# A spectral filter, a GELU block and a layer norm on one core: six filter loads instead of three ahead of the first DMA transpose, fewer throwaway matmuls, and the bias column behind the first tile's copy

## Chip, core and metric

The kernel runs on one core of a Trainium2 chip. The metric is the device time of one execution in microseconds (us). A profiled execution has a span, from its first to its last instruction, and a time of its own that is somewhat longer.

The engines are named as in the profile: PE (TensorE, matrix products, with its weight loads PEld), DVE (VectorE), ACT (ScalarE), POOL (GpSimd) and SP (SyncE, which here only issues DMAs). SBUF is the on-chip memory, PSUM the eight banks into which PE writes.

## The reference

```python
x = A_x                                  # 1 x 2048 x 640, bf16
xn = _layernorm(x, axis=-1)
return x + _A_ref(xn, A_w_r, A_w_i) + _B_ref(xn, B_w1, B_b1, B_w2, B_b2)

def _A_ref(x, w_r, w_i):                 # filter in the frequency domain
    X = jnp.fft.rfft2(x.astype(jnp.float32), axes=(-2, -1))
    X = X * (w_r + 1j * w_i)             # weights 2048 x 321
    return jnp.fft.irfft2(X, s=(S, D), axes=(-2, -1)).astype(jnp.bfloat16)

def _B_ref(x, w1, b1, w2, b2):           # 640 -> 1536 -> 640
    h = jnp.einsum("bsd,df->bsf", x, w1) + b1
    h = _gelu(h)
    return jnp.einsum("bsf,fd->bsd", h, w2) + b2
```

Both branches read the same normalized `xn`, and their sum is added to `x`.

## The kernel before

The 2048 rows are 16 tiles (c = 0 to 15) of 128 rows. Each tile is loaded (`load_x`), its mean and variance are taken on DVE (L584, L588), and the normalized tile is made on DVE (L617, into a buffer that the profile calls Z or T). Two users follow.

*The dense branch.* `xn` is needed with rows and columns exchanged (`xnT`). Tiles 0 to 3 and 5 to 7 are transposed on PE (L635) and copied out of PSUM by ACT or DVE (L496, L497). Tile 4 and tiles 8 to 15 (`BYDMA`) are transposed by a DMA that SP issues (L624). Then come the products with w1, in blocks of tiles (0), (1), (2, 3), (4 to 7), (8 to 11), (12 to 15) and 12 column groups each (`hps` in the code, L483 `ps<-xnT,W` in the profile); w1 comes in three loads (`W1P`: groups 0 to 2, 3 to 6 and 7 to 11). ACT adds the bias column `b1col` and takes the gelu (L688). The products with w2 (`ps<-W,gT`) come late in the kernel; w2 comes in four loads.

*The spectral branch* is a Fourier transform written as matrix products with tables (G, E, M, N, GE, H). The first stage uses `gtab`, the second (`bps`) `etab`, the third (`cps`) the matrix M on 32x32 tiles (`ps<-Xb,mtab`). Its results Y are copied out of PSUM by ACT and DVE, two copies each for each half, and are multiplied on DVE with the filter weights in `Wf` (four products T on L756, four sums Z on L760 for a pair of row groups). The first inverse stage (`dps`, `ps<-Z,ntab`) takes the Z; its results U are transposed by DMA (L781) into `XV`, from where the last stages run. `cps`, `dps` and the last stage's `eps` use PSUM banks 0 to 3, four at a time.

*The filter weights* come in 34 loads on SP, 17 of w_r first and then 17 of w_i. Most have 80.2 KB; the second and the third of each half have 10.0 and 70.2 KB, since one row stands alone. Every filter product on DVE waits for all 34.

*Order.* The program writes no order by hand. Each step is an operation with the engines that may do it, a price in us, a priority, what it reads and writes, and sometimes a gate (not before that step has started) or a due time `late` (not before that moment on the planner's clock). `Sched.schedule` runs through this as a list scheduler: at each point the engine that can start earliest takes, among what it can start within 0.03, the step of the highest priority. The prices and due times set the order of each engine's queue, the engine of a step that two may do, and its PSUM bank; they are not waited for on the chip. There every engine runs its queue in that order and waits for semaphores only. DMA transposes have priority 500 and more or less by a table (`DELTA`), loads on SP 400.

`load` (L478) gives the prices of DMA issues: 0.6 for a filter load, 1.0 on POOL, 0.45 for all others. The due time of the k-th filter load is

```python
late=WLATE[0] + WLATE[1] * len(B_w.writers)      # WLATE = (14.6, 0.72)
```

On SP this makes the order: loads of x, b1, w1 and G; three filter loads; the transpose of tile 4; thirteen filter loads; transposes 8 and 9; two filter loads; transposes 10 to 13; one w2 load; one filter load; transposes 14 and 15; one w2 load; the last fifteen filter loads; two w2 loads; H; then the transposes of U and the stores.

*The front.* While the first tile comes in, PE runs `WARM[0]` = 46 matmuls on zeros whose result nobody reads (`idle`, `ps<-warm`). After the five transposes of tile 0 it runs one small matmul that turns b1 into a column (`b1ps`), which ACT copies into `b1col` (L640), and `WARM[1]` = 6 more throwaway matmuls. ACT and DVE copy tile 0's transposed columns out of PSUM (`EVAC`: three fifths ACT, two fifths DVE), and block 0 of the dense branch starts.

Of the kernel before, what the change touches and what calls it, by code (L numbers as in the profile page):

```python
# [9 lines left out]
ACT = mybir.ActivationFunctionType  # L10
# [3 lines left out]
D = 640  # L14
# [4 lines left out]
NFC = 12  # L19
# [80 lines left out]
def act_us(n, ptr=0):  # L100
    return 0.055 + n / 1200.0 + 0.09 * ptr
# [277 lines left out]
W1P = ((0, 3), (3, 7), (7, 12))  # L379
GROUPS = ((0, 2), (2, 3), (5, 3), (8, 3), (11, 3), (14, 2))  # L380
BYDMA = (4, 8, 9, 10, 11, 12, 13, 14, 15)
WLATE = (14.6, 0.72)
ANY = [(0, 8)]
ZONE = {'hps': [(4, 8)], 'bps': [(0, 4), (4, 8)], 'cps': [(0, 4)], 'dps': [(0, 4)], 'eps': [(0, 4)], 'fin': [(0, 8)], 'fps': [(4, 8)], 'tps': [(0, 8)], 'aps': [(0, 8)]}
PRIO = {'hps': -118.5, 'gelu': -251.6, 'pb': 89.9, 'pc': 206.3, 'filt': 461.0, 'ipc': 165.5, 'eps': 24.1, 'fin': -47.0}
# [5 lines left out]
RES = 261.9  # L391
W2LATE = (31.0, 2.4)
HLATE = 59.8
WARM = (46, 6)
X2POS = 2
FLAG = 1.4
EVAC = {0: [((0, 3), "act"), ((3, 5), "dve")], 1: [((0, 3), "act"), ((3, 5), "dve")]}
# [2 lines left out]
def bass_parallel_sum__spectral_gfnet__dense_activation_gelu__prompt_kernel(  # L400
# [20 lines left out]
    K = Sched(nc, ["sp", "pe", "act", "dve", "pool"])  # L421
    with ExitStack() as es:
# [11 lines left out]
        ident = sb("ident", [128, 128])  # L434
# [7 lines left out]
        b1t = sb("b1t", [NFC, 128])  # L442
        b1col = sb("b1col", [128, NFC], F32)
# [11 lines left out]
        xnT = sb("xnT", [128, 5, S])  # L455
# [14 lines left out]
        def psb(slot, dims, off=0, p0=0, n=128):  # L470
            return bass.AP(tensor=PS, offset=p0 * 4096 + slot * 512 + off, ap=[[4096, n]] + dims)
# [3 lines left out]
        p_yo, p_y2, p_yf, p_os = Pool(2), Pool(1), Pool(2), Pool(4)  # L475

        def load(dst, src, buf, nbytes, after=(), reads=(), rate=395e3, q="sp", late=0.0):
            return K.op([(q, 0.6 if buf is B_w else 1.0 if q == "pool" else 0.45)], 20 if q == "pool" else 400, lambda e, _: e.dma_start(dst, src), reads=reads, writes=[buf], after=after, nbytes=nbytes, rate=rate, late=late)  # L478

        def mms(lst):  # L480
            def f(e, _):
# [5 lines left out]
        def pe(segs, prio, lst, **kw):  # L487

            o = K.op([("pe", sum(u for _, u in segs))], prio, mms(lst), alts=[segs], **kw)
            o.lst = lst  # L490
            return o
# [24 lines left out]
        B_id, B_b1, B_b2b = Buf("ident"), Buf("b1t"), Buf("b2")  # L516
# [3 lines left out]
        B_w2 = [Buf(f"w2_{j}") for j in range(4)]  # L520
        B_w = Buf("W")
# [50 lines left out]
        B_b1ps, B_b1c = Buf("b1ps", psum), Buf("b1col")  # L572
# [5 lines left out]
        for c0, n in [(0, 1), (1, 1)] + [(c, 2) for c in range(2, 16, 2)]:  # L578
            pr = 100 - c0 / 2
            B_mv, B_ve, B_r = Buf("mv"), Buf("ve"), Buf("r")  # L580
            for c in range(c0, c0 + n):
                B_st = Buf("st")
                for h in range(2):
                    st = K.op([("dve", 0.393)], pr, lambda e, _, c=c, h=h: e.bn_stats(stats[:, c, 6 * h:6 * h + 6], view(X, c * D + H2 * h, [[1, H2]])),  # L584
                         reads=[B_x[c]], writes=[B_st], gate=first_ve if c == 1 else [])
# [9 lines left out]
            else:  # L595
                K.op([("dve", 0.09)], pr, lambda e, _, a=a, b=b: e.tensor_scalar_add(ve[:, a:b], mv[:, a:b, 1], 1e-5), reads=[B_mv], writes=[B_ve])  # L596
                K.op([("pool", 0.65)], pr, lambda e, _, a=a, b=b: e.tensor_tensor(out=rstd[:, a:b], in0=ve[:, a:b], in1=mhalf[:, a:b], op=ALU.pow),  # L597
                     reads=[B_ve, B_mh], writes=[B_r])
# [3 lines left out]
        for pair in range(8):  # L602
            xn, x1, xf = Buf(f"xn{pair}", p_xn), Buf(f"xe{pair}", p_x1), Buf(f"xf{pair}", p_xf)

            def xnv(n, o, dims, xn=xn):
                return view((TT, Yb, Zb)[xn.slot // 2], xn.slot % 2 * 2 * D + n * D + o, dims)

            def x1v(o, dims, x1=x1):
                return view(TT, X1 + x1.slot * 2 * D + o, dims)

            def xfv(o, dims, xf=xf):
                return view(TT, XF + xf.slot * 2 * D + o, dims)
            for n in range(2):
                c = 2 * pair + n
                pr = 100 - c / 2
                B_xn = Buf(f"xn_{c}")
                o = K.op([("dve", 0.356)], pr, lambda e, _, c=c, n=n, xnv=xnv: e.tensor_scalar(  # L617
                    out=xnv(n, 0, [[1, D]]), in0=view(X, c * D, [[1, D]]), scalar1=mv[:, c, 0:1], scalar2=rstd[:, c:c + 1], op0=ALU.subtract, op1=ALU.mult),
                    reads=[B_x[c], B_rs[c]], writes=[xn, B_xn])
                norm_ops.append(o)  # L620
                if not c:
                    second_st.gate.append(o)
                if c in BYDMA:
                    K.op([("sp", 1.3)], 500, lambda e, _, c=c, n=n, xnv=xnv: e.dma_start_transpose(xnT[:, :, 128 * c:128 * c + 128], xnv(n, 0, [[1, D]])),  # L624
                         reads=[B_xn, xn], writes=[B_xnT[c]], nbytes=163840, rate=137e3)
                    continue
                tps = Buf(f"tps{c}", psum, 2 if c < 2 else 1, ZONE["tps"])

                def tpv(j0, j1, c=c, tps=tps):
                    over = c < 2 and j0 >= 3  # L630
                    return psb(tps.slot + over, [[1, 512]]).bitcast(BF)[:, 128 * (j0 - 3 * over):128 * (j1 - 3 * over)]

                def xt(e, _, n=n, xnv=xnv, tpv=tpv):
                    for j in range(5):
                        ins = e.transpose(tpv(j, j + 1), xnv(n, 128 * j, [[1, 128]]), ident[:])  # L635
                    return ins
                tp = K.op([("pe", 5 * mm_us(128))], pr, xt, reads=[B_xn, xn, B_id], writes=[tps], alts=[[("128", 5 * mm_us(128))]])
                if not c:
                    pe([("128", 0.1)], 200, lambda: [(psb(B_b1ps.slot, [[1, NFC]]), b1t[:], ident[0:NFC, 0:NFC], True, True)], reads=[B_b1, B_id], writes=[B_b1ps], gate=[tp])
                    K.op([("act", 0.2)], 200, lambda e, _: e.activation(b1col[:], psb(B_b1ps.slot, [[1, NFC]]), ACT.Copy), reads=[B_b1ps], writes=[B_b1c])  # L640
                    idle(WARM[1], WARM[1] * mm_us(128), gate=[tp])
                for k, (js, engs) in enumerate(EVAC[c] if c < 2 else [((0, 5), "both")]):
                    w = 128 * (js[1] - js[0])
                    K.op([x for x in (("dve", 0.066 + w / 1860.0), ("act", act_us(w))) if engs in ("both", x[0])], pr,
                         copy(lambda c=c, js=js: xnT[:, js[0]:js[1], 128 * c:128 * c + 128],
                              lambda tpv=tpv, js=js: tpv(*js).rearrange("p (j t) -> p j t", j=js[1] - js[0])),
                         reads=[tps], writes=[B_xnT[c]] + ([B_xnTp[c][k]] if c < 2 else []))
            pr = 100 - pair - FLAG
            for k, op in enumerate((ALU.add, ALU.subtract)):
                K.op([("dve", dve_us(640, 2))], pr, lambda e, _, k=k, op=op, xnv=xnv, x1v=x1v: e.tensor_tensor(  # L650
                    out=x1v(H2 * k, [[D, 2], [1, H2]]), in0=xnv(0, 0, [[D, 2], [1, H2]]), in1=xnv(0, D - 1, [[D, 2], [-1, H2]]), op=op), reads=[xn], writes=[x1])
            for k, op in enumerate((ALU.add, ALU.subtract)):
                for o_, o0, o1, w in ((128 * k, 0, H2 - 1, 128), (512 + 32 * k, 128, H2 - 129, 32)):
                    ring_ops.append(K.op([("dve", dve_us(4 * w, 2))], pr, lambda e, _, op=op, x1v=x1v, xfv=xfv, o_=o_, o0=o0, o1=o1, w=w: e.tensor_tensor(  # L654
                        out=xfv(o_, [[D, 2], [2 * w, 2], [1, w]]), in0=x1v(o0, [[D, 2], [H2, 2], [1, w]]), in1=x1v(o1, [[D, 2], [H2, 2], [-1, w]]), op=op),
                        reads=[x1], writes=[xf]))
            aps = Buf(f"aps{pair}", psum, 3, ZONE["aps"])
            for n in range(2):
                c = 2 * pair + n
                o = pe([("128", 5 * mm_us(128))], pr, lambda c=c, n=n, xfv=xfv, aps=aps: [  # L660
                    (psb(aps.slot, [[4, 64], [1, 2]], 256 * j + 2 * n), xfv(n * D + 128 * j, [[1, 128]]), gtab[:, 128 * c:128 * c + 128], True, True) for j in range(5)],
                    reads=[xf, B_g], writes=[aps])
                ring_ops.append(o)
                a_ops.append(o)
            for js in XASPLIT[pair]:
                K.op([("dve", dve_us(256 * len(js))), ("act", act_us(256 * len(js)))], pr,
                     copy(lambda pair=pair, js=js: view(XV, 2048 * js[0] + 4 * pair, [[2048, len(js)], [32, 64], [1, 4]]),
                          lambda aps=aps, js=js: psb(aps.slot, [[256, len(js)], [4, 64], [1, 4]], 256 * js[0])),
                     reads=[aps], writes=[B_xa[pair]])
# [3 lines left out]
        for bi, (c0, nt) in enumerate(BLOCKS):  # L673
            for fc in range(NFC):
# [4 lines left out]
                pr = PRIO["hps"] - bi - fc / 20  # L679
                w = [j for j, (a, b) in enumerate(W1P) if a <= fc < b][0]  # L680
                part_ = []
                for k, js in enumerate(((0, 1, 2), (3, 4))):
                    part_ = [pe([("128", len(js) * mm_us(128 * nt))], pr + 0.01 * len(part_), lambda c0=c0, nt=nt, fc=fc, hps=hps, js=js: [
                        (psb(hps.slot, [[1, 128 * nt]]), view(W1, F * j + 128 * fc, [[1, 128]]), xnT[:, j, 128 * c0:128 * (c0 + nt)], j == 0, j == 4) for j in js],
                        reads=[B_w1s[w]] + (B_xnTp[c0][:k + 1] if c0 < 2 else B_xnT[c0:c0 + nt]), writes=[hps], gate=part_)]
# [4 lines left out]
                    reads=[hps, B_b1c], writes=[bg])  # L690
# [18 lines left out]
        for gi, (c0, n) in enumerate(GROUPS):  # L709
# [4 lines left out]
                reads=B_xa + [B_e], writes=[bps, xb]))  # L714
# [9 lines left out]
        for P in range(4):  # L724
# [28 lines left out]
            for pair, Y, TB, Z in zip(two, Ys, TBs, Zs):  # L753
                pr = PRIO["filt"] - pair / 5
# [23 lines left out]
            for pair, U, B_u in zip(two, Us, B_us):  # L778
                for qq in range(2):
                    q = 2 * pair + qq  # L780
                    K.op([("sp", 1.3)], 500, lambda e, _, q=q, qq=qq, U=U, uv=uv: e.dma_start_transpose(  # L781
                        XV[:, :, 128 * q:128 * q + 128], uv(U, D * qq, [[1, D]])), reads=[U, B_u], writes=[B_v[q]], nbytes=163840, rate=137e3)

        for a, b in zip(CHAIN, CHAIN[1:]):
# [117 lines left out]
```

## Time and profile before

| | |
|---|---|
| median of 6 runs | 152.68 us (152.45 to 152.8) |
| profiled execution, its own time | 152.8 us |
| its span | 151.0 us |
| PE busy in the span | 144.5 us, 96% |
| DVE, ACT, POOL busy | 114.2, 80.9, 9.3 us |
| chain that ended last | PE 77%, DMA 8%, DVE 4%, SP queue 4%, ACT 3% |
| HBM read and written | 10.96 MB and 2.62 MB |

"Busy" of PE counts each matmul to a modelled end, and matmuls overlap, so 96% isn't a peak rate. The chain that ended last is followed back from the last instruction: at each step to what released it, or to the instruction before it on its engine; "issue" is time for which the profile shows no releaser. In a timeline a row is a run of equal instructions: start, length, engine, line, instruction, what it writes and reads, shape, how many, and in brackets the idle time before it and what ended that. SPq rows are DMA issues: their length is the time SP takes to issue, not the transfer; "us to landing" is from the issue to the completion.

### The profile page before, as it was taken

Reading aid. Unit: us, or ns where it says so; the run is one execution under the profiler, and the core shown is the slowest. Engines: PE = TensorE matmul, PEld = TensorE weight load, DVE = VectorE, ACT = ScalarE, POOL = GpSimd, SP = SyncE. Lnnn points to the kernel's source line nnn. Section 1 sums busy time; section 2 is a strip of 40 time slices with the busy share of each in tenths; the row PEclk is TensorE's granted clock in tenths of the full one; section 3 lists DMA queues with packets and bytes.
Section 4 is the critical chain, followed back from the end, with each engine's and each line's share of the span. In section 5 each row is a group of like instructions: output and inputs, shape, how many; then the busy total and the mean of one; then the engine's idle time right before and its main releaser. Section 6 shows DMA issues by size and latency. Waiting matters only on the chain.

```text
span 151.0 us, 4079 instructions
## 1 busy us (share of the span) xinstructions
PE 144.5 (96%) x1725; PEld 87.9 (58%) x1725; DVE 114.2 (76%) x244; ACT 80.9 (54%) x143; POOL 9.3 (6%) x22
## 2 busy tenths in 40 slices
PE   7989799999999997999999999999999999999993
PEld 7879697545556352355354455555667665655563
DVE  1999988999933569497999999942489998656433
ACT  3689979766886779678999471230124204100000
POOL 1120341124000000000000000000000000000000
PEclk9999999999999999999999999999999999999999
DMA  4999966658997575094006406205200232202022
GB/s 135 360 401 384 217 149 133 135 123 126 228 221 161 120 219 208 0 82 96 7 0 82 96 4 121 57 20 119 42 0 3 88 130 87 87 4 105 25 87 87
DMA packets 29610, 17.93 MB, mean 119 GB/s; under 512 B 18425, under 2 KB 28281, under 8 KB 29593
## 3 DMA queue, kind: packets, MB, share of 16 engines
q1 hardware_dynamic: 28552, 16.47, 43.7%
q0 software_dynamic: 240, 0.69, 1.7%
q10 hardware_dynamic: 800, 0.52, 1.2%
q8 instruction: 13, 0.21, 0.6%
q14 instruction: 5, 0.03, 0.1%
HBM read 10.96 MB, written 2.62 MB: 90 GB/s over the span
## 4 chain that ended last, share of the span: by engine, by line
PE 77%; DMA 8%; DVE 4%; SPq 4%; ACT 3%; issue 1%
PE ps L483 77%; DMA W<-in_B_w_dram 8%; SPq L478 4%; DVE T L756 2%; ACT gT L688 1%; DVE Z L760 1%; ACT T L496 1%; ACT U L496 1%; DVE Y L497 1%; DVE xnT L856 0%; ACT Y L496 0%; PE ps L635 0%; DVE W L865 0%
## 5 line engine op out<-in xcount | busy, mean ns | idle before, releaser
L483 PE MATMUL ps<-xnT,W 128*128 128x512 bf16 (+2 forms) x360 | 56.5, 308 | 1.4 <-DMA W<-in_B_w_dram 1.2
L483 PE MATMUL ps<-W,gT 128*128 128x512 bf16 (+3 forms) x396 | 56.0, 295 | 0.1
L483 PEld LDWEIGHTS ps<-W,gT 128*128 128x128 bf16 x396 | 30.1, 98 | 22.6 <-issue 1.2
L483 PEld LDWEIGHTS ps<-xnT,W 128*128 128x128 bf16 x360 | 28.8, 98 | 22.2 <-issue 2.1
L688 ACT ACTIVATE gT<-ps,b1col 128x512 bf16<-128x512 f32 (+2 forms) x72 | 36.3, 552 | 6.7 <-PE ps L483 6.2
L496 ACT ACTIVATE Wf<-ps 128x960 bf16<-128x960 f32 (+1 forms) x8 | 7.0, 902 | 23.7 <-PE ps L483 23.7
L584 DVE BATCH_NORM_STATS2 stats<-X 128x6 f32<-128x320 bf16 x32 | 14.1, 470 | 2.3 <-DMA X<-in_A_x_dram 2.3
L756 DVE TENSOR_TENSOR T<-Y,Wf 128x1288 bf16<-128x1288 bf16 x16 | 12.3, 822 | 1.2 <-DMA Wf<-in_A_w_i_dram 1.2
L496 ACT ACTIVATE Xb<-ps 128x960 bf16<-128x960 f32 (+1 forms) x9 | 9.8, 1138 | 2.8 <-PE ps L483 2.6
L811 DVE TENSOR_TENSOR Wf<-Wf 128x960 bf16<-128x960 bf16 (+1 forms) x12 | 6.7, 598 | 5.7 <-PE ps L483 5.5
L496 ACT ACTIVATE XV<-ps 128x1280 bf16<-128x1280 f32 (+1 forms) x8 | 9.3, 1157 | 1.5 <-PE ps L483 1.5
L496 ACT ACTIVATE U<-ps 128x512 bf16<-128x512 f32 (+1 forms) x14 | 5.4, 448 | 8.0 <-PE ps L483 8.0
L496 ACT ACTIVATE Y<-ps 128x644 bf16<-128x644 f32 x10 | 6.9, 713 | 3.1 <-PE ps L483 3.1
L654 DVE TENSOR_TENSOR T<-T 128x512 bf16<-128x512 bf16 (+1 forms) x32 | 8.5, 315 | 0.1
L865 DVE TENSOR_TENSOR W<-ps,X 128x640 bf16<-128x640 f32 (+2 forms) x10 | 6.7, 687 | 2.2 <-PE ps L483 2.2
L865 DVE TENSOR_TENSOR W<-ps,xnT 128x640 bf16<-128x640 f32 x8 | 6.5, 816 | 1.9 <-PE ps L483 1.9
L597 POOL TENSOR_TENSOR rstd<-ve,mhalf 128x2 f32<-128x2 f32 (+1 forms) x8 | 5.9, 736 | 27.1 <-DVE ve L596 27.1
L806 DVE TENSOR_TENSOR Wf<-Wf 128x960 bf16<-128x960 bf16 (+1 forms) x12 | 6.9, 596 | 0.9 <-ACT Wf L496 0.7
L483 PE MATMUL ps<-getab,XV 32*128 32x160 bf16 (+1 forms) x128 | 7.5, 241 | 0.0
L483 PE MATMUL ps<-etab,XV 32*128 32x160 bf16 (+1 forms) x128 | 7.2, 232 | 0.3 <-ACT T L496 0.3
L497 DVE CAST Y<-ps 128x644 bf16<-128x644 f32 x6 | 5.0, 827 | 3.2 <-PE ps L483 3.2
L483 PEld LDWEIGHTS ps<-etab,XV 32*128 32x128 bf16 (+1 forms) x128 | 5.5, 95 | 3.0 <-ACT T L496 0.8
(58 smaller groups left out, 124.7 us busy)
## 6 DMA issues: line engine op xcount, KB each, us to landing
out_dram<-W SPq DMA_DIRECT2D x15, 160.0 KB, 1.8
X<-in_A_x_dram SPq DMA_DIRECT2D x7, 320.0 KB, 8.2
W<-in_B_w_dram SPq DMA_DIRECT2D x4, 480.0 KB, 4.5
Wf<-in_A_w_r_dram SPq DMA_DIRECT2D x15, 80.2 KB, 3.1
Wf<-in_A_w_i_dram SPq DMA_DIRECT2D x15, 80.2 KB, 3.1
W<-in_B_w_dram SPq DMA_DIRECT2D x1, 800.0 KB, 6.4
W<-in_B_w_dram SPq DMA_DIRECT2D x1, 640.0 KB, 11.8
gtab<-c_G SPq DMA_DIRECT2D x1, 512.0 KB, 7.2
```

The costliest lines, as they stand in the source:

```text
L478: return K.op([(q, 0.6 if buf is B_w else 1.0 if q == "pool" else 0.45)], 20 if q == "pool" else 400, lambda e, _: e.dma_start(dst, src), ...
L483: ins = e.matmul(o_, lhsT=lw, rhs=rh, start=st, stop=sp_, skip_group_check=True)
L496: return e.activation(dst(), src(), ACT.Copy, scale=scale)
L497: return e.tensor_copy(dst(), src())
L584: st = K.op([("dve", 0.393)], pr, lambda e, _, c=c, h=h: e.bn_stats(stats[:, c, 6 * h:6 * h + 6], view(X, c * D + H2 * h, [[1, H2]])), rea ...
L597: K.op([("pool", 0.65)], pr, lambda e, _, a=a, b=b: e.tensor_tensor(out=rstd[:, a:b], in0=ve[:, a:b], in1=mhalf[:, a:b], op=ALU.pow), read ...
L654: ring_ops.append(K.op([("dve", dve_us(4 * w, 2))], pr, lambda e, _, op=op, x1v=x1v, xfv=xfv, o_=o_, o0=o0, o1=o1, w=w: e.tensor_tensor(ou ...
L688: K.op([("act", act_us(128 * nt, 1))], pr + PRIO["gelu"], lambda e, _, c0=c0, nt=nt, fc=fc, hps=hps: e.activation(gT[:, fc, 128 * c0:128 * ...
L756: filt_ops.append(K.op([("dve", dve_us(4 * KP, 2))], pr, lambda e, _, k=k, Y=Y, TB=TB, pair=pair: e.tensor_tensor(out=view(TT, TB.slot * 8 ...
L806: K.op([("dve", dve_us(320 * n, 2))], pr + 2, lambda e, _, k=k, op=op, yo=yo, y2=y2, n=n: e.tensor_tensor(out=view(Wf, Y2 + y2.slot * 3 * ...
L811: K.op([("dve", dve_us(320 * n, 2))], pr + 3, lambda e, _, k=k, op=op, y2=y2, yf=yf, n=n: e.tensor_tensor(out=view(Wf, YF + yf.slot * 3 * ...
L865: K.op([("dve", dve_us(w))], 95, lambda e, _, os_=os_, fps=fps, o0=o0, w=w, xov=xov, shaped=shaped, base=base: e.tensor_tensor(out=shaped( ...
```

## The change

It gives the filter loads earlier due times (13 and 0.5 apart), and new prices: 0.645 for a filter load and now also for a w2 load, 0.47 for other loads on SP, 1.33 for a DMA transpose. The throwaway matmuls go from 46 and 6 to 43 and 5. The bias matmul and its copy on ACT are gated on the start of the first copy of tile 0 out of PSUM, in place of the start of tile 0's transposes, so that they are queued behind it.

```diff
-WLATE = (14.6, 0.72)
+WLATE = (13, 0.5)
...
-WARM = (46, 6)
+WARM = (43, 5)
...
         def load(dst, src, buf, nbytes, after=(), reads=(), rate=395e3, q="sp", late=0.0):
-            return K.op([(q, 0.6 if buf is B_w else 1.0 if q == "pool" else 0.45)], ...
+            return K.op([(q, 1.0 if q == "pool" else 0.645 if buf is B_w or buf in B_w2 else 0.47)], ...
...
                 if c in BYDMA:
-                    K.op([("sp", 1.3)], 500, lambda e, _, ...: e.dma_start_transpose(xnT[...], xnv(...)),
+                    K.op([("sp", 1.33)], 500, lambda e, _, ...: e.dma_start_transpose(xnT[...], xnv(...)),
...
                 if not c:
-                    pe([("128", 0.1)], 200, lambda: [(psb(B_b1ps.slot, [[1, NFC]]), b1t[:], ...)], reads=[B_b1, B_id], writes=[B_b1ps], gate=[tp])
-                    K.op([("act", 0.2)], 200, lambda e, _: e.activation(b1col[:], ...), reads=[B_b1ps], writes=[B_b1c])
                     idle(WARM[1], WARM[1] * mm_us(128), gate=[tp])
                 for k, (js, engs) in enumerate(EVAC[c] if c < 2 else [((0, 5), "both")]):
                     w = 128 * (js[1] - js[0])
-                    K.op([x for x in (("dve", ...), ("act", act_us(w))) ...], pr, copy(...), reads=[tps], ...)
+                    ev = K.op([x for x in (("dve", ...), ("act", act_us(w))) ...], pr, copy(...), reads=[tps], ...)
+                    if not c and not k:
+                        pe([("128", 0.1)], 200, lambda: [(psb(B_b1ps.slot, [[1, NFC]]), b1t[:], ...)], reads=[B_b1, B_id], writes=[B_b1ps], gate=[ev])
+                        K.op([("act", 0.2)], 200, lambda e, _: e.activation(b1col[:], ...), reads=[B_b1ps], writes=[B_b1c])
...
                     q = 2 * pair + qq
-                    K.op([("sp", 1.3)], 500, lambda e, _, ...: e.dma_start_transpose(
+                    K.op([("sp", 1.33)], 500, lambda e, _, ...: e.dma_start_transpose(
```

## The prediction

> **What bounds the kernel now.** The profiled execution took 152.8 us, its span is 151.0 us, so 1.8 us lie outside the span; the six runs have a median of 152.68. I read the chain that ended last first, because it says which engine carries the end and where it had to stop.
>
> ```profile
> 6.96 0.04 issue
> 7.00 11.83 DMA W<-in_B_w_dram
> 18.83 0.14 issue
> 18.97 3.64 PE ps L483 x48
> 22.61 0.56 PE ps L635 x10
> 23.17 36.02 PE ps L483 x355
> 59.19 1.10 issue
> 60.28 14.65 PE ps L483 x242
> ```
>
> TensorE (PE) carries the end. Up to 18.83 the chain is one load: the middle part of w1 (640 KB), issued at 7.00 behind all loads of x and landing 11.83 us later. From 18.97 PE never stops until 59.19, stands 1.10 us, and goes on. An idle microsecond of PE counts in full only after 18.97; anything won before it is eaten by the wait for that load. So the next view is the timeline around 59.19 (start, length, engine, line, instruction, idle before it and who ended it).
>
> ```profile
> 52.66 0.83 DVE L497 CAST Y<-ps 128x644 bf16<-128x644 f32 x1 [0.78 <-PE ps L483]
> ...
> 54.66 2.31 DVE L756 TENSOR_TENSOR T<-Y,Wf 128x1288 bf16<-128x1288 bf16 x3 [1.17 <-DMA Wf<-in_A_w_i_dram]
> ...
> 56.88 0.89 DVE L760 TENSOR_TENSOR Z<-T 128x644 bf16<-128x644 bf16 x2
> ...
> 57.69 0.82 DVE L756 TENSOR_TENSOR T<-Y,Wf 128x1288 bf16<-128x1288 bf16 x1
> ...
> 57.93 1.25 PE L483 MATMUL ps<-xnT,W 128*128 128x512 bf16 x5
> ...
> 58.55 0.90 DVE L760 TENSOR_TENSOR Z<-T 128x644 bf16<-128x644 bf16 x2
> ...
> 59.36 0.82 DVE L497 CAST Y<-ps 128x644 bf16<-128x644 f32 x1
> ...
> 60.28 0.52 PE L483 MATMUL ps<-Z,ntab 32*32 32x320 bf16 x32 [1.10 <-issue]
> ```
>
> The chain names no releaser for the PE wait, but the rows do: the waiting matmuls (the first inverse ones, `dps0_0`) start 0.10 after the DVE cast at 59.36 ends (60.18). That cast empties the four PSUM banks they need, and it stands on DVE behind eight back-to-back filter instructions, whose first stood 1.17 us idle until the last filter weight landed. So the PE stop of 1.10 is the landing of the last filter load, handed on through DVE. Why that load is late stands in SyncE's (SP's) timeline.
>
> ```profile
> 7.48 3.62 SPq L478 DMA_DIRECT2D Wf<-in_A_w_r_dram  x3
> 16.54 1.32 SPq L624 DMA_TRANSPOSE xnT<-Z  x1
> 17.90 9.45 SPq L478 DMA_DIRECT2D Wf<-in_A_w_r_dram  x13
> ...
> 42.11 10.56 SPq L478 DMA_DIRECT2D Wf<-in_A_w_i_dram  x15
> ```
>
> SP is idle from 11.10 to 16.54, because the DMA transpose next in its queue waits for the normalized tile (DVE L617, 16.07 to 16.51). After 16.54 every row starts 0.04 to 0.05 after the one before, up to 54.36: SP itself is what makes the last filter load late.
>
> **Part 1, three filter loads into SP's idle stretch.** The planner takes due times and prices only to fix the order. Following its arithmetic by hand with 0.47 for a load, 0.645 for a filter or W2 load, 1.33 for a transpose and due times 13 + 0.5 k, SP's order becomes: six filter loads, transpose 4, twelve, transposes 8 and 9, two, transposes 10 to 13, W2, transposes 14 and 15, W2, fourteen, then as before. It was three, one, thirteen, two, two, four, W2, one, two, W2, fifteen. A filter load takes SP 0.60 (median of the rows) and 0.04 between rows: three of them are 1.92 us that move from the busy stretch into the idle one. They fit in 5.44 us even at the longest row seen (1.92 each, 5.76) but for some 0.4 us. Everything behind them on SP comes earlier: transposes 8 to 13 by one load (0.64), 14 and 15 by two, the last filter load and the two W2 loads after it by three (1.92). The transposes' inputs are there: the closest is tile 10, normalized at 30.59 while SP comes at 30.68.
>
> The last filter load landed 0.08 before the DVE row at 54.66; it would land at about 52.66. DVE can use only what it waits: 1.17 us, since its cast before ends at 53.49. This leaves 0.75 us of the 1.92 as a margin. The whole DVE sequence and the PE start move 1.17 earlier, to 59.11; PE's own work before it (57.93, 1.25 us) ends at 59.18, and following groups start some 0.08 before that modelled end (50.87 + 1.25 against 52.05). So the stop goes, and what is late next is PE's own work. The profile counts the stop as 1.10, the start can move 1.17; I take 1.10. The ends are 0.7 (the landing moves by 0.7 only, if SP stalls 1.2 us more on a full queue, about what its 1.92 us row is over the median) and 1.17.
>
> **Part 2, what the three loads push aside.** They queue behind the w1 load that lands at 18.83, which PE waits for (0.92 us idle at 18.97). Loads issued from SP at 7.48 landed after it, 9.3 to 9.8 us and more after their issue, so the SP queue keeps its order and w1 should not move. But its last packets share the 16 DMA engines with more filter packets than before. No row shows this; a gain is excluded, as nothing ahead of it goes. From above: three loads are 241 KB, and at the 191 GB/s of the stretch 17 to 19 us this is 1.26 us if all of it went in front. I take 0.05, near the queue's order, and keep 0 to 1.26. Transpose 4 (4.0 us from issue to landing, 20.5) may come up to 1.26 later; its tile is first read at 24.53, so 4 us cover it. The same holds for etab (POOL, issued 15.68, 4.1 us to landing), read at 45.32. On POOL's queue nothing is passed.
>
> **Part 3, the front: four throwaway matmuls fewer, bias column moved.** The first transposes on PE start at 5.67, straight behind the throwaway ones, while their tile is ready at 5.34. Three fewer give them 0.165 us (0.055 each at that point). On ACT the bias copy (6.25, 0.18) goes behind the first tile's copy (6.33), which then can follow the dummy activation of 5.97 at about 6.05: block 0 starts on PE at about 6.6 in place of 6.87. The bias column is ready at about 6.7, before the first gelu needs it (7.1), so its cover is the first three matmul groups; without that cover it would cost the copy, 0.18. All of it ends at the wait for w1's third part (PE idle 0.27 before 8.96) and once more at 18.97. Worth nothing.
>
> The matmul rate decides if this holds. In the profile's stretches PE began 20 matmuls in 1.00 to 3.00 and 24 in 3.00 to 5.30, 0.1 us each, but 15 in 6.90 to 7.80, all with a granted clock of 1.00; the quick spacing begins about 4.3 us after the first matmul, and 43 at 0.106 reach 5.45, just past it. If the quick rate came late, 20 matmuls before 8.2 would take 0.05 more each, 1.0 us, of which the waits before 8.96 and the 0.92 at 18.97 take all or nearly all. So 0, at most 0.1.
>
> The Trainium skill ("TensorE: Matmul & The Clock Gate", Part 1) speaks against cutting so close: it gives a release after about 3.4 us of sustained work, but through a free-running window, so that the number of slow matmuls changes from run to run. By its 3.4 us even 32 matmuls would do and the cut is free; by its changing window the quick rate may come later in some runs. The trace's 4.3 us lies between, and the sum is the same by either.
>
> **Part 4, the other prices** (W2 0.645, loads 0.47, transposes 1.33) change planned times by hundredths. They reorder SP as said; on PE, ACT and DVE only a near tie could turn, and I keep their orders. The trace shows no cost of a turned order: from below -0.3, from above 2.0, as in rival (c). After 60 us PE's stops (0.26 at 80.42, 0.06 at 97.20) are fed by PE's own results through ACT and DVE and move along; SP has been free since 54.36 when the second transposes begin (63.47).
>
> **Sum.** 152.8 - 1.10 + 0.05 = 151.75 for a profiled execution. That execution stood 0.12 above the median, so the median goes to 151.6.
>
> **Rivals.** (a) The gain stays away: the queue of loads is full, SP stalls and the landing hardly moves. For it: two issues of 1.39 and 0.95 in place of 0.60 from 21.12 on, and the one of 1.92 at 7.48. Against: from 23.5 to 51 the filter rows stand at 0.60, so SP and not the queue sets the pace there. With a landing 0 to 0.3 earlier the time is 152.4 to 152.7. (b) Slower: w1's last packets are held by the added ones. Place: PE's wait at 18.97. From there all PE work moves, but the stop at 59.19 gives up to 1.17 back, so the time is above the old one when w1 lands more than 1.17 later (after 20.0), and measurably so after 20.3. At 1.26 it is 152.8; at three times the spacing of the next two filter landings (21.17 and 21.73; 1.7 in all) it is 152.68 - 1.17 + 1.7 = 153.2. For it: 17 to 19 us moved only 191 GB/s at a DMA share of 1.25; against: first come, first served on SP. (c) The planner, priced anew, swaps PSUM banks or groups on PE. The price runs from a small gain (-0.3, the stop at 80.42) to both long stops once more (0.92 + 1.10 = 2.0): 151.3 to 153.6. For it: orders follow from priorities and due times that near ties decide; against: Part 4.
>
> **How the numbers follow.** The measurement tells 0.2% (0.31 us) from no change. Forecast: 0.67, with its own range 151.2 to 152.1. (a) 0.09, (b) 0.12, (c) 0.12. Faster by over 0.31: the forecast, 0.02 of (a), 0.02 of (c), together 0.71. Within: 0.07 of (a), 0.04 of (b), 0.03 of (c), 0.14. Slower: 0.08 of (b), 0.07 of (c), 0.15. The range runs from 151.1 (a gain of 1.5: the 1.17, and the 0.26 stop with it) to 152.9: it holds the forecast with its ends, (a), and what of (b) and (c) isn't slower, 0.86 in all.
>
> **What would show it.** Right: SP's timeline has six filter loads before the transpose at about 16.5 and ends its first part near 52.4; the DVE row L756 starts near 53.4 without a DMA wait; no PE stop of a microsecond near 59; PE's wait at 18.97 stays near 0.92. Wrong: the wait at 18.97 grows by more than 0.3, the DVE wait for the filter stays, or PE has a new stop whose releaser is an evacuation.

## The result: slower by 0.6%, and the profile after

The changed kernel takes 153.86 us (median of 21 runs, 152.95 to 156.07), the kernel before 152.75 us (44 runs, 152.27 to 154.85). The ratio is 1.0063, with a 95% interval of 1.0046 to 1.0080: slower, where 151.6 was forecast, and outside the range of 151.1 to 152.9. The medians are of all runs; the ratios leave out the runs, most over 155 us, in which the profile shows a lower granted clock and a time well above the others of the same kernel.

The profiled execution after took 153.66 us with a span of 151.9 us, against 152.8 and 151.0 before. The chain that ended last (start, length, what) shows both places that the prediction spoke of:

```profile
6.63 0.04 issue
6.68 13.14 DMA W<-in_B_w_dram
19.81 0.14 issue
19.95 3.64 PE ps L483 x48
23.59 0.56 PE ps L635 x10
24.15 36.03 PE ps L483 x355
60.17 0.77 issue
60.95 5.11 PE ps L483 x103
```

The load of w1's middle part went out 0.32 earlier than before and landed 0.98 later (19.81 for 18.83). PE's wait for it grew from 0.92 to 1.69, and all PE work behind moved by 0.98. The stop near 60 shrank only from 1.10 to 0.77, which gives 0.33 back. What is left, 0.65, is seen at the stop's end (60.95 for 60.28, 0.67). By 81.30 the lag is 0.88, and the span ends 0.9 later; what adds the last 0.2 between 61 and 76 us was not followed further.

The other two views, DVE and PE around the stop, and SP's issues, in the timeline after:

```profile
53.65 0.83 DVE L497 CAST Y<-ps 128x644 bf16<-128x644 f32 x1 [0.78 <-PE ps L483]
...
55.32 2.31 DVE L757 TENSOR_TENSOR T<-Y,Wf 128x1288 bf16<-128x1288 bf16 x3 [0.85 <-ACT gT L689]
...
60.03 0.82 DVE L497 CAST Y<-ps 128x644 bf16<-128x644 f32 x1
...
60.95 0.52 PE L483 MATMUL ps<-Z,ntab 32*32 32x320 bf16 x32 [0.77 <-issue]
```

```profile
7.16 5.62 SPq L478 DMA_DIRECT2D Wf<-in_A_w_r_dram  x6
16.75 1.31 SPq L624 DMA_TRANSPOSE xnT<-Z  x1
18.11 8.02 SPq L478 DMA_DIRECT2D Wf<-in_A_w_r_dram  x11
...
42.05 8.96 SPq L478 DMA_DIRECT2D Wf<-in_A_w_i_dram  x14
```

SP did as foretold: six filter loads stand before the transpose, and the last filter load landed at 52.98 in place of 54.58. DVE's first filter product (L757, L756 before) no longer waits for that load. It is nevertheless idle for 0.85 before 55.32, and the row names ACT.

### The profile page after: what moved, and what is told of

Its sections match the earlier page's. It is cut to its first block, busy times and chain, and to the rows that moved or that the text cites. A ratio compares the mean times of both kernels' runs of the same rounds, so it can differ in the third digit from the quotient of the medians.

```text
span 151.9 us, 4072 instructions
## 1 busy us (share of the span) xinstructions
PE 144.9 (95%) x1721; PEld 88.1 (58%) x1721; DVE 114.2 (75%) x244; ACT 81.1 (53%) x143; POOL 9.3 (6%) x22
## 3 DMA queue, kind: packets, MB, share of 16 engines
q1 hardware_dynamic: 28552, 16.47, 47.0%
## 4 chain that ended last, share of the span: by engine, by line
PE 77%; DMA 9%; DVE 4%; SPq 4%; ACT 3%; issue 1%
PE ps L483 77%; DMA W<-in_B_w_dram 9%; SPq L478 4%; DVE T L757 2%; ACT gT L689 1%; DVE Z L761 1%; ACT T L496 1%; ACT U L496 1%; DVE Y L497 1%; DVE xnT L857 0%; ACT Y L496 0%; PE ps L635 0%; DVE W L866 0%
## 5 line engine op out<-in xcount | busy, mean ns | idle before, releaser
L757 DVE TENSOR_TENSOR T<-Y,Wf 128x1288 bf16<-128x1288 bf16 x16 | 12.3, 823 | 0.9 <-ACT gT L689 0.8
```

What stands on the lines that cost most here:

```text
L757: filt_ops.append(K.op([("dve", dve_us(4 * KP, 2))], pr, lambda e, _, k=k, Y=Y, TB=TB, pair=pair: e.tensor_tensor(out=view(TT, TB.slot * 8 ...
```

## Experiments: which edit, and which wait

Theory A: the three added filter loads hold the last packets of w1's middle load, and what remains of DVE's wait is the work of waiting itself, the steps through 34 semaphores. Rival B: the edits of the front (fewer throwaway matmuls, bias column) cost the time. Rival C: the rest of DVE's wait belongs to what its row names, ACT, or to the landing, and not to the semaphores. Four kernels ran side by side.

**The front alone (front_only).** The kernel before with these lines of the change:

```diff
-WARM = (46, 6)
+WARM = (43, 5)
...
+                    if not c and not k:
+                        pe([("128", 0.1)], ..., writes=[B_b1ps], gate=[ev])
```

> The kernel before with the front edits alone (43 and 5 throwaway matmuls, bias column behind the first copy); three filter loads ahead of transpose 4 as before. Theory A (the three added filter loads push w1's middle part, which PE waits for): no change, ratio 0.999 to 1.001, PE wait for w1 near 19.0 stays 0.8 to 1.0. Rival B (the front edits start the dense branch late): slower by about 0.6%, and the wait for w1 grows or the work before it ends later.

Measured: 152.94 us, ratio 1.0002 [0.9980, 1.0023]; w1's middle load landed at 18.43. The rows of PE behind that load and of DVE's first filter product:

```profile
18.57 1.69 PE L483 MATMUL ps<-xnT,W 128*128 128x256 bf16 x14 [0.45 <-DMA W<-in_B_w_dram]
```

```profile
53.94 1.57 DVE L757 TENSOR_TENSOR T<-Y,Wf 128x1288 bf16<-128x1288 bf16 x2 [0.84 <-ACT gT L689]
```

The front costs nothing and brings nothing, within 0.2%; rival B falls. The second row shows more: with the order of loads of before, DVE was idle for 0.84 and PE's stop near 60 was 0.77, as in the kernel after. In this execution SP's last filter issue had no stall (it started at 50.40, in before at 51.15 and took 1.53), and the last filter load landed at 53.48, 0.46 before DVE's product.

**The six loads and the prices alone (six_only)**, with the old front:

```diff
-WLATE = (14.6, 0.72)
+WLATE = (13, 0.5)
...
-            return K.op([(q, 0.6 if buf is B_w else ...
+            return K.op([(q, ... 0.645 if buf is B_w or buf in B_w2 else 0.47)], ...
```

> The changed kernel with the old front (46 and 6 throwaway matmuls, bias column as before): six filter loads ahead of transpose 4 and the new prices alone. Theory A: slower by 0.5 to 0.7%, w1's middle part lands near 19.8 in place of 18.8, the filter stop of PE near 60 is 0.7 to 0.8 in place of 1.1. Rival B: the time of the kernel before within 0.2%.

Measured: 153.59 us, ratio 1.0049 [1.0024, 1.0074]; w1 landed at 19.95, and the stop near 60 was 0.78. PE's row behind that load:

```profile
20.09 0.60 PE L483 MATMUL ps<-xnT,W 128*128 128x256 bf16 x4 [1.74 <-DMA W<-in_B_w_dram]
```

The slowdown is in the six loads and the prices; that it is the loads, the next section shows.

**One semaphore in place of 34.** Before, each filter load has a semaphore of its own, and DVE's first product waits for all of them. Here all 34 loads count up one semaphore (16 each), and DVE waits once for 544:

```diff
+        wsem = nc.alloc_semaphore("d_w")
...
+                if o.nbytes and o.writes and o.writes[0].name == "W":
+                    o.sem, o.count = wsem, 16 * 34
...
-                    for d in o.waits:
-                        e.wait_ge(d.sem, d.count)
+                    for s_, c_ in {(d.sem, d.count): 0 for d in o.waits}:
+                        e.wait_ge(s_, c_)
```

In the kernel before (one_sem_before):

> The kernel before with one semaphore for all 34 filter loads (waited for once, at 544) in place of 34 semaphores. Theory A says that most of the 1.17 us in which DVE stands before the first filter product is its own 17 semaphore steps of 0.098 us; but the last filter load lands at 54.58, which is later than those steps but for 0.3 us, so here the product starts when the load lands and the time stays within 0.2%. If the semaphore steps cost nothing: no change either. It is the partner of the next run.

and in the kernel after (one_sem_after):

> The changed kernel with one semaphore for all filter loads. Theory A: the last filter load lands near 53, before the cast ahead of the products ends (54.5), so without the 17 semaphore steps the first product starts about 0.85 us earlier, right behind that cast; the PE stop near 60 (0.77) goes, and the time falls by 0.6 to 0.8 us, to that of the kernel before within 0.2%. Rival C (the stop near 60 is the filter load's landing, as predicted): no change against the changed kernel, 0.6% slower than before.

Measured in the kernel before: 152.44 us, ratio 0.9980 [0.9958, 1.0001]; the last filter load landed at 54.04, DVE started its product at 54.13 after an idle 0.53, PE's stop was 0.47. In the kernel after: 153.16 us, ratio 1.0024 [0.9998, 1.0049] against the kernel before; the load landed at 52.59, and DVE (start, length, line, instruction) went on without a wait:

```profile
53.49 0.83 DVE L500 CAST Y<-ps 128x644 bf16<-128x644 f32 x1 [0.78 <-PE ps L486]
54.24 2.30 DVE L760 TENSOR_TENSOR T<-Y,Wf 128x1288 bf16<-128x1288 bf16 x3
```

The product starts 0.75 after its cast, where the kernel after has 1.67 (53.65 to 55.32). PE's stop near 60 is gone, though ACT's work is the same, so rival C falls. The time fell by less than foretold: 0.43 us against the kernel with six loads that ran beside it (153.16 for 153.59), where 0.6 to 0.8 was expected, and it stayed 0.24% above the kernel before, with an interval that holds no difference. What the stop of after was made of stands in the list of instructions of the wait's line, between 52 and 56 us (line, engine, instruction, count, shortest/median/longest in ns, first and last start). First the kernel before:

```profile
L361 DVEq EVENT_SEMAPHORE  x17: 49/50/374, 52.7 to 54.2; - x17
```

then the kernel after:

```profile
L361 DVEq EVENT_SEMAPHORE  x17: 49/50/50, 53.7 to 55.2; - x17
```

DVE's sequencer handles 17 such instructions one after the other, two semaphores in each, from 53.7 to 55.2, about 0.1 us apart, also when all of them have long been reached. Before, only one of the 17 waited: the longest, 0.374 against 0.05. So, in this execution, of the 1.17 that the row before gave to the DMA, 0.33 was the landing (54.66 against 52.66 + 1.67 = 54.33) and 0.84 the steps. The trace of before held this; the timeline of DVE alone, which leaves semaphore instructions out, did not.

## Experiments: why w1 lands later

The loads of w1 and of the filters are issued in the same order on the same queue, w1 first. Theory A, now in its plain form: any bytes and packets queued behind w1 hold its end. Theory N: it is where the filter loads write. Each goes to 16 partitions, 8 rows of 642 bytes in each. Theory B here: up to three loads are drained beside w1 for nothing, and only more pile up.

**No filter load ahead of the transpose (none_ahead).** One edit, `WLATE = (16.7, 0.6)` in the kernel before.

> The kernel before with no filter load ahead of the first DMA transpose (its three follow the transpose, the rest of SP's order the same). Only two numbers are wanted: where w1's middle load lands, and where the last filter load lands. Theory A (the loads queued behind w1 hold its last packets, about 0.35 us a load, as 18.83 to 19.81 for three more): w1 lands at 17.7 to 17.9, PE's wait near 19 goes. Theory B (three loads are drained beside w1 without harm, only more than three pile up): w1 stays at 18.4 to 18.8, the wait at 0.5 to 0.9. Both: the last filter load lands 1.9 later, at about 56.5, DVE's first product starts at 56.6, and the end comes 1.9 later than before, 154.6 us, whatever w1 does, since PE's stop near 60 absorbs it.

Measured: w1 landed at 18.05, between the two theories' figures and nearer to A. So already the three loads of before cost w1 some 0.3 to 0.9 (in the four that have three ahead, before, front_only, one_sem_before and the later one_sem_w2_late, it landed at 18.83, 18.43, 18.95 and 18.34). The end came out differently than expected: the last filter load landed at 55.61 (not 56.5), since SP's last filter issue ended only 0.98 later (53.66 for 52.68). The one run took 153.82 us. And PE's wait came back in another place. The timeline row of PE:

```profile
35.73 0.60 PE L483 MATMUL ps<-xnT,W 128*128 128x512 bf16 x2 [0.89 <-DMA xnT<-Z]
```

That is the DMA transpose of tile 11, landed at 35.68: PE, freed of its wait at 19, runs into the next transfer. Already before, that one was nearly late: it landed at 35.32, and PE's work behind it stands 0.28 earlier there than here (DVE's cast at 52.66 against 52.94), so PE came to it at about 35.45, 0.13 after its landing.

**Three loads more that nobody reads, narrow and wide.** The kernel before with three loads of 82 KB between w1 and the first filter load, into the still empty buffer of w2 (whose own loads wait for them). Narrow (narrow_extra):

```diff
+            scr.append(load(bass.AP(tensor=W2, offset=32 * k * NFC * D, ap=[[2 * NFC * D, 16], [321, 8], [1, 321]]),
+                            bass.AP(tensor=A_w_r.tensor, ..., ap=[[128 * 321, 16], [321, 8], [1, 321]]), ...
```

> The kernel before, its filter loads where they were, and three loads more of the same 82 KB between w1's middle load and the first filter load, that nobody reads: each goes to 16 partitions in 8 pieces of 642 bytes, as a filter load does, into the still empty buffer of w2. Theory A and Theory N (it is the narrow destination that holds w1): w1 lands at 19.6 to 19.9, PE's wait near 20 is 1.6 to 1.8, PE's stop near 60 0.7 to 0.9, time 153.6 to 153.8 (ratio 1.005). If six filter loads cost for another reason (order, which loads they are): 18.4 to 18.9 and 152.8.

and wide (wide_extra):

```diff
+            scr.append(load(bass.AP(tensor=W2, offset=k * 321, ap=[[NFC * D, 128], [1, 321]]),
+                            bass.AP(tensor=A_w_r.tensor, ..., ap=[[321, 128], [1, 321]]), ...
```

> As narrow_extra, but each of the three loads of 82 KB goes to all 128 partitions, one piece of 642 bytes in each: the same bytes and the same number of packets. Theory A (bytes and packets behind w1): the same as the narrow ones, w1 at 19.6 to 19.9, 153.6 to 153.8. Theory N (16 partitions are written by all engines at once, and that slows the packets): w1 at 18.5 to 19.0, PE's wait 0.5 to 1.0, time 152.6 to 152.9.

Measured: narrow 153.30 us, ratio 1.0037 [1.0011, 1.0064], w1 at 19.66, PE's wait 1.67; PE's stop near 60 was 1.17, not 0.7 to 0.9, for the last filter load landed only at 55.48 there. Wide 153.04 us, ratio 1.0008 [0.9975, 1.0041], w1 at 18.96. This speaks for Theory N, but the pair had a flaw: in the narrow loads the eight rows touched each other, and their packets turned out to have 5136 bytes, not 642. So both ran once more (narrow_642, wide_642), the narrow one with its rows 1288 bytes apart (`[644, 8]` in place of `[321, 8]`):

> As narrow_extra, but the eight rows of each of the three loads go 1288 bytes apart in their 16 partitions, as in a filter load, so that their packets have 642 bytes; in narrow_extra the rows touched, and the packets had 5136 bytes. Theory N (it is the 16 partitions): w1 lands at 19.6 to 19.9, PE's wait near 20 is 1.6 to 1.8, time 153.3 to 153.7. If 5136 bytes were what held w1 there: 18.5 to 19.0, as wide_extra, 152.7 to 153.0.

> The kernel of wide_extra once more, beside narrow_642 on the same chip, to see if its landing holds: the same bytes, packets of 642 bytes and count of packets as narrow_642, into 128 partitions instead of 16. Theory N: w1 at 18.5 to 19.0, at least 0.6 before narrow_642, time 152.7 to 153.0. Theory A (bytes and packets): the same landing as narrow_642 within 0.2.

Measured: narrow 153.53 us, ratio 1.0046 [1.0023, 1.0069], w1 at 20.11, PE's wait 1.84. Wide 152.96 us, ratio 1.0010 [0.9984, 1.0035], w1 at 18.84; its profiled execution took 155.2 us, so the rows below are of the other wide run. The chain of narrow_642, to set beside that of after:

```profile
7.02 13.09 DMA W<-in_B_w_dram
20.11 0.14 issue
20.25 3.64 PE ps L483 x48
```

In the four kernels with three filter loads ahead w1 landed at 18.34 to 18.95, 18.64 in the mean; in the three with six ahead (after, six_only, one_sem_after) at 19.81, 19.95 and 19.66. The same bytes more in the same number of packets of the same size make it land 1.47 later than that mean if they go to 16 partitions, and 0.2 to 0.3 later if they go to 128, about where the latest of the four lies. The stretches say how (us, length, busy time of five engines with counts, PE clock, DMA share, GB/s). The kernel after:

```profile
16.00:17.00 1.00, 1.00 (x11) 0.90 (x10) 1.00 (x5) 0.85 (x3) 0.59 (x1) 1.00 1.19 225
17.00:18.00 1.00, 1.00 (x18) 0.96 (x17) 1.00 (x5) 0.93 (x3) 0.00 (x0) 1.00 1.31 154
```

narrow_642:

```profile
16.00:17.00 1.00, 1.00 (x12) 0.90 (x10) 1.00 (x5) 0.91 (x2) 0.74 (x2) 1.00 1.15 251
17.00:18.00 1.00, 1.00 (x17) 0.95 (x15) 1.00 (x4) 0.87 (x3) 0.00 (x0) 1.00 1.26 223
```

wide_extra:

```profile
16.00:17.00 1.00, 1.00 (x12) 0.89 (x10) 1.00 (x5) 0.85 (x3) 0.92 (x2) 1.00 1.13 326
17.00:18.00 1.00, 1.00 (x14) 0.91 (x12) 1.00 (x5) 0.88 (x2) 0.00 (x0) 1.00 0.95 162
```

The DMA engines are equally busy in the first row, but move 225 and 251 GB/s narrow and 326 wide: each packet takes longer. Between 16.5 and 17.0 the trace has 109 packets of 642 bytes at 74 ns each in the mean in after, 110 at 67 ns in narrow_642, and 218 at 36 ns in wide_extra. And w1 has only its last few packets left by then: from 17.0 to 18.3 before shows 7 to 10 of them (1024 bytes) in each half microsecond, 48 to 56 ns each, about the pace of a single engine. In after it is 3 or 4 in a half microsecond, at 95 to 142 ns each. The steps of w1's semaphore, which counts to 16, say the same: before, fifteen have come by 17.64 and the last comes at 18.83; in after by 18.07 and at 19.81; with no filter load ahead by 17.00 and at 18.05. So in these three the last sixteenth of w1 alone makes the landing. One late engine fits that; which engine carries a packet, the trace doesn't say.

The Trainium skill ("SBUF — State Buffer", "Door 1: The DMA port swizzle") has a reason: 32 neighbouring partitions are reached through 8 of SBUF's 16 DMA ports, and it measures 189 GB/s there against 328 for all 128 partitions, with 1 MiB. A filter load's 16 partitions lie within 32. The 225 and 251 GB/s against 326 in the first row here lie in the same direction, with a smaller gap; that ports are the cause, no run here shows by itself.

**The same packets in half-wide loads (halves_after).** The kernel after with one semaphore, and four of its filter loads cut as eight loads of one row into 64 partitions:

```diff
+            for r in range(0 if ri else 8):
+                load(bass.AP(tensor=Wf, offset=2 * KP * r, ap=[[2 * WP, 64], [1, 321]]),
+                     bass.AP(tensor=wsrc.tensor, ..., ap=[[16 * 321, 4], [128 * 321, 16], [1, 321]]), ...
```

> The kernel after with one semaphore for all filter loads (as one_sem_after) and four of the loads ahead of the first transpose, which write 16 partitions and 8 rows each, cut another way: eight loads of one row into 64 partitions each, the same packets of 642 bytes. Eleven loads (eight of 41 KB and three as before, 492 KB in all, 82 KB more than the six) then stand ahead of the transpose. Theory N (the narrow destination holds w1's last packets): w1 lands at 18.8 to 19.2 in place of 19.66, PE's wait is 0.9 to 1.3 in place of 1.77, span 150.0 to 150.4 (one_sem_after: 150.8), time 152.3 to 152.7. Theory A (bytes and packets behind w1): w1 at 19.8 to 20.2, span 151.0 to 151.3, time 153.3 to 153.6.

Measured: w1 landed at 18.08, earlier than either theory said, as if nothing stood behind it. But the test is less clean than it was meant to be: the filter packets came at 64 to 68 in each half microsecond and 33 ns each, 4.3 to 4.5 engines' worth, so most engines were left to w1. That agrees with the Trainium skill ("DMA: Bandwidth & Descriptors", "Why a DMA increments its semaphore by 16 and not by 1"), by which a DMA uses the largest number of engines, up to 16, that divides the outermost sizes of both sides, 64 and 4 here: four. The first transpose, too, was issued only behind w1's landing. The time was 152.88 us, ratio 1.0004 [0.9979, 1.0029]: of the 1.58 won on w1 most was lost again, for SP took up to 1.71 for a load, issued that transpose at 18.22, and PE waited 1.16 for the transpose of tile 11 at 36.07.

One thing is not told apart. The wide loads of 82 KB also read one run of memory, the narrow ones 16 pieces. The half-wide loads read 64 pieces and their packets were quick, which speaks for the destination; a run with a wide destination and a scattered source on all engines was not made.

## Experiments: a version that beats both

**One semaphore and w2 out of the way (one_sem_w2_late).** The two w2 loads that stand on SP before the last filter loads are first read at 81 us.

```diff
-W2LATE = (31.0, 2.4)
+W2LATE = (50.0, 1.0)
```

> The kernel before with one semaphore for all filter loads (as one_sem_before) and the two w2 loads that stood on SP between the filter loads put behind the last filter load (w2 is first read at 81 us). If DVE's remaining wait of 0.53 in one_sem_before is the landing: the last filter load lands at about 52.8 in place of 54.04, DVE's first product starts at 53.5 to 53.6 without a wait, PE's stop near 60 (0.47) goes, span 150.0, time 151.9 to 152.1 (ratio 0.994 to 0.996). If the transposes behind come late by it or something else holds PE near 60: 152.4, as one_sem_before.

Measured: 151.67 us (4 runs), ratio 0.9918 [0.9886, 0.9950], span 149.5; better than foretold. The last filter load landed at 51.59, DVE's product started at 53.02, 0.74 after its cast (52.28), with no wait, and PE's stop is gone. In this execution w1 also landed early (18.34, with three loads ahead), which the edit doesn't explain.

**Everything together (spread_pool).** To the one semaphore and the late w2 loads of the version before: no filter load ahead of the first DMA transpose, none between the transposes, and the last eight on POOL's queue, with a semaphore of their own.

```diff
-WLATE = (14.6, 0.72)
+WLATE = (16.7, 0.6)
...
+                 B_w, ..., q="pool" if len(B_w.writers) >= 26 else "sp",
+                 late=40.0 if len(B_w.writers) >= 26 else 16.7 + 0.6 * len(B_w.writers) if len(B_w.writers) < 13 else 36.5)
...
+                    o.sem, o.count = (wpool, 16 * 8) if e == "pool" else (wsem, 16 * 26)
```

> A version meant to beat both: no filter load ahead of the first DMA transpose, none between the transposes 8 to 15, the last eight filter loads on POOL's queue from 37 us on, the w2 loads behind them, one semaphore for each of the two queues' filter loads. Expected: w1 lands at 18.0 as in none_ahead, PE's wait near 19 goes; transpose 11 lands at 34.7 instead of 35.68 there, so PE's wait of 0.89 at 35.73 stays away; the last filter load lands before 52.5, DVE's first product follows its cast; no stop near 60. Span 149.0 to 149.3, time 150.8 to 151.1 (ratio 0.988 to 0.990). Against it: the transposes, not the load, may set PE at 35.7 again (151.3), or loads on POOL's queue may land late and hold DVE (152 or more).

Measured: 151.11 us (151.03 to 151.47), ratio 0.9885 [0.9860, 0.9910]. SP's timeline and DVE's:

```profile
6.68 0.43 SPq L481 DMA_DIRECT2D W<-in_B_w_dram  x1
16.67 1.30 SPq L628 DMA_TRANSPOSE xnT<-Z  x1
18.02 9.14 SPq L481 DMA_DIRECT2D Wf<-in_A_w_r_dram  x13
27.21 5.25 SPq L628 DMA_TRANSPOSE xnT<-Z  x4
```

```profile
51.97 0.83 DVE L500 CAST Y<-ps 128x644 bf16<-128x644 f32 x1 [0.78 <-PE ps L486]
52.72 2.30 DVE L760 TENSOR_TENSOR T<-Y,Wf 128x1288 bf16<-128x1288 bf16 x3
```

w1 landed at 18.02, the transpose of tile 11 at 33.85, and neither PE's wait near 19, nor that at 35.73, nor the stop near 60 is left. POOL issued its eight loads in 0.53 to 0.67 each from 35.65 on; the last of them landed at 45.74, and SP's last at 51.82. Expected and measured agree, but for the transpose of tile 11, which landed 0.85 earlier than foretold. The intervals of this version and of the one before it overlap a little; what each of its three further edits is worth alone was not measured.

## Why the prediction was wrong, by its own steps

**SP's order and the landing (Part 1, first half): right.** Order, idle stretch and the three loads moved are as worked out; the landing came 1.60 earlier (54.58 to 52.98), of 1.92. Rival (a) falls with that. One reading did not hold: the transposes of tiles 8 to 13, foretold 0.64 earlier, went out 0.26 to 0.48 later (27.66 for 27.40, 31.59 for 31.32, 34.45 for 33.97), for tile 8 was normalized only at 27.64, 0.98 later, with the work behind w1.

**What the landing is worth (Part 1, second half): wrong, 1.10 taken, 0.33 measured.** The step that failed is "So the PE stop of 1.10 is the landing of the last filter load, handed on through DVE." The row said "1.17 <-DMA Wf", and a row's idle time is put down to whatever came last. The wait on 34 semaphores was never costed; 0.84 of the 1.17 was there with or without the landing. Even the 0.33 belongs to the profiled execution of before: in front_only, with the same order of loads, the landing held nothing (idle 0.84, stop 0.77), so earlier loads could win 0 to 0.33. The lower end of this term, 0.7, was taken from the landing alone and could not hold this. That PE follows DVE's cast was right: with DVE's wait at zero the stop is gone (one_sem_after).

**The push on w1 (Part 2): the mechanism was named, the term mis-sized: 0.05 taken, 0.98 measured**, inside the ends of 0 and 1.26. The step that failed is "I take 0.05, near the queue's order". "First come, first served on SP" holds for the issue and for the order of landings, not for the speed of the packets: the wide loads show w1 nearly unharmed in the same queue, the narrow ones a microsecond late. The row that spoke for it, 191 GB/s between 17 and 19 us at a DMA share of 1.25, was the better guide: the end of 1.26 worked out from it was nearer to the truth than the value taken (with the loads' 82,176 bytes each it is 1.29).

**The front (Part 3): right in its worth.** Worth 0; alone it measures 1.0002. The path was to be block 0 at about 6.6 on PE. In front_only it is 6.65. In after, the five transposes of tile 0 on PE do start earlier (5.59), but take 0.71 in place of 0.44, and block 0 starts at 6.89 for 6.87: the quick spacing came only at 6.5 in this execution, where before had it at 5.4. So the risk that Part 3 named came true, and the waits behind took it, as it said. The granted clock of 1.00 that Part 3 read ahead of the quick spacing is no measurement: the trace's record of the clock begins at 5.42 in before and at 6.51 in after, where the spacing changes.

**Orders and other prices (Part 4): right.** The other engines kept their orders but for the front's edits, so rival (c) falls.

**The sum.** 152.8 + 0.98 - 0.33 + 0.2 = 153.65, against 153.66; the 0.2 is a remainder read off the profile after, so it isn't a test. In the chances, 0.67, 0.09, 0.04 and 0.05 add up to 0.85, not 0.86. Of the rivals, (b) named the place and the cause. Its condition, w1 more than 1.17 late, wasn't met and wasn't needed, since it counted on the 1.17 of DVE to be given back; with 0.33 the point of no gain lies at 0.33. So the 0.12 given to (b) was too little for two reasons: the push was taken as unlikely, and the point from which it decides was put too far out.

## What to carry to other kernels

Before a wait is put down to the load that came last, count the semaphores that the waiting instruction takes: here 34 of them cost DVE 0.84 us of a wait of 1.17, and one shared semaphore, waited for at its full count, took it away. A load queued behind another can still delay it, here when it wrote few partitions from scattered rows; leave an idle issue stretch ahead of a critical load's landing idle, or fill it with loads that write many partitions (no version here won time by filling it). When a wait is removed, look for the next transfer that was just in time: the transpose of tile 11 had some 0.1 us to spare before, and with w1 at 18.05 and 18.08 (none_ahead, halves_after) PE waited 0.89 and 1.16 for it.

## What the runs showed of the hardware

- DVE's wait on 34 semaphores was paid with one instruction for two semaphores, 0.098 us apart (17 in 1.66 us, 53.66 to 55.32), even if all are reached; the product then starts 1.67 after its cast in place of 0.75.
- Three loads of 82 KB into 16 partitions each, issued behind a load of 640 KB on the same queue, made it land 1.0 to 1.5 later (19.66 and 20.11, against 18.34 to 18.95, 18.64 in the mean, without them); into 128 partitions 0.2 to 0.3 later than that mean (18.84, 18.96).
- The profile's row of the hardware queue shows it at a glance: the same 28552 packets and 16.47 MB took 43.7% of the 16 engines' span before and 47.0% after.
- A load of 64 rows into 64 partitions from a source with an outer size of 4 moved at 4.3 to 4.5 engines' worth (64 to 68 packets of 33 ns in 0.5 us). The semaphore's updates say four: 520 in all, which is 16 for each of the thirty other loads and 5 for each of these eight, one at the end of the issue and four more.
- PE's quick matmul spacing began between 2.7 and 5.5 us after the first matmul, by the execution's record of the clock (wide_642 at 3.69; before 5.42; after and narrow_642 6.51; the first matmul is at 0.99 to 1.00 in all).
